# Decode attention over a sliding window: V of two slabs fetched by one DMA with 65536-byte rows, its products on 64 weight columns, and the second slab's softmax run at once

## The chip, the cores and the metric

The kernel runs on one core of one Trainium2 chip. The metric is the device time of one execution in microseconds (us). Before the change it is 362.82 us, the median of 3 runs (362.75 to 362.86). The profile shown here is of one execution of its own, which took 363.02 us.

## The reference, cut to what matters

Two independent problems A and B of the same shape are computed and their outputs laid side by side. Each is one decode step of attention with a sliding window.

```python
B, Sq, D = 2, 1, 576
Hq, Hkv, Sk, Dh = 32, 16, 16384, 128
W = min(4096, max(256, Sk // 4))                 # 4096: only the last 4096 keys count
q = (x @ wq).reshape(B, Sq, Hq, Dh).transpose(0, 2, 1, 3)
k = jnp.repeat(k_cache[:, :, Sk - W:, :], 2, axis=1)
v = jnp.repeat(v_cache[:, :, Sk - W:, :], 2, axis=1)
scores = jnp.einsum("bhqd,bhkd->bhqk", q, k) * (Dh ** -0.5)
p = softmax(scores, axis=-1)
o = jnp.einsum("bhqk,bhkd->bhqd", p, v)
return o.transpose(0, 2, 1, 3).reshape(B, Sq, Hq * Dh) @ wo
# out = concatenate([problem A, problem B], axis=-1)
```

All tensors are bf16. One head's window of K (or V) is 4096 x 128 x 2 bytes = 1 MiB, and each problem has 2 x 16 heads of K and as many of V, so 128 MiB of cache are read for one query row of each head. The rest that is read are wq and wo, 4.5 MiB each for each problem.

## The kernel before, in words

**Slabs and groups.** The work is cut into 16 slabs (ND, eight for each problem). A slab holds four heads, `[g::SPP]` of the 32 (line 246): 4 MiB of K and 4 MiB of V, each fetched by one DMA into one slot of the tile ring (128 partitions, four slots of 32768 bytes in a partition). A partition gets 128 consecutive positions times 128 elements of one head, which are 32768 consecutive bytes of the cache: one row of the DMA. Two slabs, 2G and 2G+1, make a group G.

**The stream.** All large transfers are issued by SP, in the order of the list stream (lines 216 to 223), and each waits for the reader of the slot that it overwrites (`reader[n - NR]`, four transfers back). SP issues in order, so a transfer that waits holds up those behind it. Before, the order is Q0, Q1 (the wq of the two problems), K0, K1, V0, K2, V1, ..., K13, V12, K14, K15, V13, V14, V15. V15 comes in two pieces (PIECES: 3 MiB and 1 MiB). wo comes in parts that are issued ahead of a named transfer (w_at, line 226): part 0 (all of problem A) ahead of K5, part 1 ahead of V11, part 2 ahead of V12; part 3 and the small last pieces (issue_last) behind V15.

**One slab.** The names of the steps are those of the code, with s for the slab and u = 0..3 for a quarter of it:

- X(s,u), DVE, line 515: a transpose of a quarter of the K slab into xt, which has NKT = 3 buffers; X(s,u) therefore waits for the S that read the buffer three quarters ago. X(s,3) frees the slot of K.
- S(s,u), PE, lines 540 and 188: eight matmuls of 512 columns into the scores' PSUM tile ST[s % 2], which ACT has filled with a mask before (fill, line 415).
- max, Tm, nM, nMrep, bias, bcp, exp (lines 550, 553, 563, 568, 573, 579, 585): the maximum of the slab, turned and spread by two tiny PE transposes, then one ACT exponential into pR, with the sums in rsum.
- pC, DVE, line 593: a transpose of pR into the weights of the V product. It waits for fill(s+2) and exp(s).
- PV, PE, line 631: 32 matmuls of 512 columns, each with 32 weight columns (128 x 32 of the array), four of them on the four column quarters of the array at a time, into ACC. It needs V of the slab and pC.
- rsel (POOL), tot (PE), rsb (DVE): 1/sum of a group. accev (ACT, line 643), accm, acca, accr (POOL), comb (PE), norm, spread (DVE): fold ACC into the group's output. redist, rev, proj (PE, ACT, PE, lines 739, 757, 786): the product with wo.

**The order within an engine** is the order in which the loop at lines 849 to 890 adds the steps; every engine works strictly in that order. In it, the softmax of slab s-1 is laid between the quarters of slab s: max(s-1) behind X(s,0), Tm behind S(s,0), nM ahead of X(s,2), bias and exp ahead of X(s,3), pC(s-1) behind X(s,3), PV(s-1) behind S(s,3). S(s,3) waits for pC(s-1) (line 529). After the loop (lines 891 to 923) come the last slab's softmax between pieces of PV13, then PV14, comb, norm and proj of group 6 in two steps, PV15 in its two pieces, and the output.

**The start.** wq of both problems arrives, the queries of all eight groups are computed (q, qrow, qtr, qkeep), and only then X(0,0) runs, since DVE does the qtr of all groups first.

Of the kernel before, what the change touches and what calls it, by code (L numbers as in the profile page):

```python
# [59 lines left out]
def build_kernel(nc, probs, out, cfg=None):  # L60
    cfg = dict(cfg or {})
    NR = cfg.get("NR", 4)
    NKT = cfg.get("NKT", 3)
    NPT = cfg.get("NPT", 3)
    LS = 1
# [48 lines left out]
    with es:  # L114
# [25 lines left out]
        pR = sb("pR", [128, 1024], BF16)  # L140
        pC = sb("pC", [128, NPT, NJ, 8], BF16)
# [22 lines left out]
        acc_r = sb("acc_r", [128, 2, 128], BF16)  # L164
        o_rest = sb("o_rest", [Bb, NB1], FP32)
        ident_r = sb("ident_r", [128, 32], BF16)
        out_A = sb("out_A", [Bb, NOUT], BF16)
        out_sb = [out_A[:, :], pR[0:Bb, 0:NOUT]]
# [11 lines left out]
        wo_sem = [sem("wo%d" % r) for r in range(2)]  # L180
# [30 lines left out]
        p_zq = S.add("dve", lambda e: e.memset(zq[:].rearrange("d p z w -> d (p z w)").bitcast(FP32), 0.0), [], "zero_zq")  # L211
        p_ones_f = S.add("dve", lambda e: e.memset(ones_f[:], 1.0), [], "ones_f")
# [4 lines left out]
        for s_ in range(ND + LS):  # L217
            if s_ < ND:
                stream.append(("K", s_))
            if s_ >= LS and s_ != ND - 2:  # L220
                if s_ == ND - 1:
                    stream.append(("V", ND - 3))
                stream.append(("V", s_ - LS))
        pos = {key: n for n, key in enumerate(stream)}
        w_at = {}
        for part, at in ((0, ("K", 5)), (1, ("V", 11)), (2, ("V", 12))):
            w_at.setdefault(at, []).append(part)

        slab_dma = {}
# [9 lines left out]
        def issue_slab(n):  # L239
# [4 lines left out]
            P, g = D_ // SPP, D_ % SPP  # L244
            src_t = probs[P][1] if kind == "K" else probs[P][2]
            src = src_t.rearrange("b h s d -> (b h) s d")[g::SPP, Sk - W:Sk, :].rearrange("c (r j) d -> r c (j d)", r=32)
            r = n % NR
            deps = [reader[n - NR]] if n >= NR else []
# [10 lines left out]
        def issue_wq(n, P):  # L259
            wqP = probs[P][3]  # L260
            r = n % NR
            deps = [reader[n - NR]] if n >= NR else []
# [9 lines left out]
        def issue_last(woP, lo, r0, deps):  # L272
            for n_, hs in enumerate(HEADS):
                def f(e, n_=n_, hs=hs):
                    t, r = divmod(hs[0], 2)
                    row = t * HH + r0 + 256 + 128 * r
                    return e.dma_start(wob[:, lo + 4 + hs[0]:lo + 4 + hs[0] + len(hs), :],
                                       woP[row:row + 128 * len(hs), :].rearrange("(h d) n -> d h n", d=128)).then_inc(wl_sem[n_], 16)
                wo_last.append(dma_op("sp", wl_sem[n_], 1, f, deps, "wl%d" % n_))

        def issue_wo(part):
# [3 lines left out]
                (16, 8, 1024, 1, [proj.get(5)], (6,)),  # L285
                (24, 4, 1536, 1, [proj.get(7)], (7,)))[part]
            assert None not in deps
            woP = probs[P][4]
            sem_ = wo_sem[lo // 16]
            src = woP.rearrange("(t r) n -> t r n", t=2)[:, r0:r0 + 64 * n, :].rearrange("t (p s) n -> p t (s n)", s=n)  # L290
# [4 lines left out]
            if part == 3:  # L295
                issue_last(woP, lo, r0, deps)
# [48 lines left out]
        def init_small():  # L345
# [15 lines left out]
                mask4S[:], ident_b[:].rearrange("d (a s) -> d s a", s=4), AX.X, ALU.max), [p_ident_b], "mask4S")  # L361
            init["maskJ"] = S.add("dve", lambda e: e.tensor_reduce(
# [48 lines left out]
        def do_fill(s):  # L411
            deps = [init["maskB"], zqev[s]]
# [11 lines left out]
        def do_qpair(i):  # L424
# [14 lines left out]
            for g in range(2):  # L439
                def fn(e, part=todo_[(0, ends[0])[g]:ends[g]]):  # L440
                    last = None
                    for ch, b in part:
                        c0 = (b % 2) * HH + 512 * (Gs[b // 2] % GPP)
                        w_ = ring[:, nq % NR, ch * HD + c0:ch * HD + c0 + 512] if ch < NFC else wqr[:, P, c0 - (b % 2) * HH:c0 - (b % 2) * HH + 512]
# [63 lines left out]
        def do_X(s, u):  # L508
# [4 lines left out]
            if i >= NKT:  # L513
# [3 lines left out]
                ring[:, n % NR, :].bitcast(FP32).rearrange("k (j q w) -> k q j w", q=4, w=64)[:, u]),  # L517
# [4 lines left out]
        def do_S(s, u):  # L522
# [5 lines left out]
            if u == NU - 1 and 1 <= s < ND - 1:  # L528
                deps.append(chain[(s - 1, "pC")])
# [42 lines left out]
        def do_exp(s):  # L572
# [8 lines left out]
            if s >= 1:  # L581
                d.append(chain[(s - 1, "pC")])
            if s >= 2:
                d.append(chain[(s // 2 - 1, "rsel")])
            chain[(s, "exp")] = S.add("act", lambda e: e.activation(  # L585
                pR[:, :], ST[s % 2][:, :], ACTF.Exp, bias=bias_sb[:, 0:1], scale=SCALE,
                accum_out=rsum[:, s % 2:s % 2 + 1]), d, "exp%d" % s)

        def do_pC(s):
            d = [chain.get((s + 2, "fill")), chain[(s, "exp")]]  # L590
            if s >= NPT:
                d.append(PVop[s - NPT])
            chain[(s, "pC")] = S.add("dve", lambda e: e.transpose(  # L593
                pC[:, s % NPT, :, :].rearrange("k j c -> k (j c)"), pR[:, :]), d, "pC%d" % s)

        def do_rsel(G):
            d = [chain[(2 * G, "exp")], chain[(2 * G + 1, "exp")], init["maskS"]]
# [20 lines left out]
        def do_PV(D_, rounds, wait):  # L618
# [4 lines left out]
            if rounds[0] == 0 and D_ >= 1:  # L623
                deps.append(acc_ev[D_ - 1])

            def f(e):
                last = None
                for jr in rounds:
                    for cb in range(4):
                        j0_ = JR * jr + 4 * cb  # L630
                        last = e.matmul(ACC[32 * cb:32 * cb + 32, 0:512],  # L631
                                        pC[:, D_ % NPT, j0_:j0_ + 4, :].rearrange("k j c -> k (j c)"),
                                        ring[:, n % NR, j0_ * 128:(j0_ + 4) * 128],
# [5 lines left out]
            if rounds[-1] == last_r:  # L639
                d = [op]  # L640
                if D_ >= 2:
                    d.append(acc_r_ev[D_ - 2])
                acc_ev[D_] = S.add("act", lambda e: e.activation(acc_sb[:, D_ % 2, :], ACC[:, :], ACTF.Copy), d, "accev%d" % D_)  # L643
                G = D_ // 2
                if not by_group(G) or (D_ % 2 == 0 and G < NG - 2):
                    return
                l0, l1 = (0, 2) if G < NG - 2 else (D_ % 2, D_ % 2 + 1)
                a_ = acc_sb[:, l0:l1, :]
                v = a_.rearrange("k l (j d) -> k l j d", j=4)
                t = S.add("pool", lambda e: e.tensor_tensor(  # L650
                    v, v, maskJ[:].unsqueeze(1).unsqueeze(3).broadcast_to([128, l1 - l0, 4, 128]), ALU.mult),
                    [acc_ev[2 * G + l] for l in range(l0, l1)] + [init["maskJ"]], "accm%d" % D_)
                t = S.add("pool", lambda e: e.tensor_tensor(a_[:, :, 0:256], a_[:, :, 0:256], a_[:, :, 256:512], ALU.add),  # L653
                          [t], "acca%d" % D_)
                d = [t]
                if G >= 1:
                    d.append(comb[2 * G - 1])
                t = S.add("pool", lambda e: e.tensor_tensor(
                    acc_r[:, l0:l1, :], a_[:, :, 0:128], a_[:, :, 128:256], ALU.add), d, "accr%d" % D_)
                for l in range(l0, l1):  # L660
                    acc_r_ev[2 * G + l] = t

        def do_comb(D_):
            if by_group(D_ // 2):
# [3 lines left out]
                def fg(e, bank):  # L668
                    last = None
                    for l_ in range(2):  # L670
                        last = e.matmul(bank[:, 8 * l_:8 * l_ + 8], acc_r[:, l_, :], maskS[:, :], start=True, stop=True)
                    return last
                n, bank, comb[D_] = tb_job(fg, "comb%d" % D_, [acc_r_ev[D_ - 1], acc_r_ev[D_], init["maskS"]])
# [10 lines left out]
        def do_norm(D_):  # L684
# [5 lines left out]
            if by_group(G):  # L690
# [3 lines left out]
                def f_nm(e):  # L694
                    last = None
                    for l_ in range(2):
                        last = e.tensor_tensor(
                            oTg[u % 2][:, 0:16 * nG].rearrange("d (b g l r t) -> d g l b t r", b=Bb, g=nG, l=2, r=2)[:, G - g0, l_],
# [6 lines left out]
                nk, mD = {4: (4, "maskA"), 2: (8, "mask16D"), 1: (16, "maskD")}[nG]  # L705
                mask_ = {"maskA": maskA, "mask16D": mask16D, "maskD": maskD}[mD]
                deps = [norm[D_], init[mD]]
                if u >= 2:
                    deps.append(redist[u - 2])
                spread[u] = S.add("dve", lambda e: e.tensor_tensor(  # L710
                    om[:, u % 2, :].rearrange("d (h k t) -> d h k t", k=nk, t=2),
# [312 lines left out]
```

## Time and profile before

| what | value |
|---|---|
| median of 3 runs | 362.82 us |
| the profiled execution | 363.02 us |
| its span, first to last instruction | 361.8 us |
| time around the span | 363.02 - 361.8 = 1.2 us |
| bytes read | 153.10 MB |
| busy: PE, DVE, ACT, POOL | 60%, 56%, 19%, 10% |
| mean granted TensorE clock | 0.882 |

How to read it: busy times are shares of the span; the row DMA of the page gives in 40 slices of 9.05 us how busy the core's 16 DMA engines were, in tenths. In a timeline a row is: start in us, length in us, engine, line, operation, tiles, shapes and count, and in brackets the idle time of the engine just before it and what ended that idle time. The chain of waits is the sequence of steps that ended last, followed back from the last instruction. Matmuls overlap, so that rows of one matmul each start about 0.22 us apart at full clock and about 0.43 us apart at half clock, though each lasts 0.38 us or 0.63 us.

### The profile page before, as it was taken

What the parts mean: (1) busy time and instruction counts of PE and PEld (TensorE: products, weight loads), DVE (VectorE), ACT (ScalarE), POOL (GpSimd) and SP (SyncE); (2) the same over time, 40 slices, a digit from 0 to 9 for tenths busy, and PEclk for the clock granted to TensorE, in tenths of its full rate; (3) what the DMA queues carried; (4) which work ended last, traced back from release to release, by engine and by line L of the source; (5) the groups of instructions that cost most, each with busy time, mean ns of one, the idle gap of its engine ahead of it and who ended that gap; (6) DMA issues with size and microseconds to landing.
All of it is one profiled execution on the core that took longest, in us unless ns stands there. A gap on an engine that the chain in (4) does not pass through costs nothing.

```text
span 361.8 us, 2730 instructions
## 1 busy us (share of the span) xinstructions
PE 218.6 (60%) x1318; PEld 55.8 (15%) x945; DVE 200.9 (56%) x175; ACT 68.2 (19%) x149; POOL 35.3 (10%) x55
## 2 busy tenths in 40 slices
PE   0399195763747207466574737766867707657786
PEld 0010021120111101112120201212121201211132
DVE  4112599846647019283756658392919239079931
ACT  1036502130203002103020203020201203002131
POOL 1000000004000400001300040002100040200020
PEclk9999689997889857969698978899898978969999
DMA  8999999999999999999999999999999999999996
GB/s 348 421 449 406 464 406 437 431 408 453 415 442 438 428 424 438 429 428 438 417 446 422 435 428 442 426 435 428 424 424 440 431 424 433 431 438 428 438 409 248
DMA packets 6491, 153.27 MB, mean 424 GB/s; under 512 B 712, under 2 KB 1232, under 8 KB 1616
## 3 DMA queue, kind: packets, MB, share of 16 engines
q1 hardware_dynamic: 6476, 153.10, 98.8%
q8 instruction: 9, 0.15, 0.2%
q14 instruction: 2, 0.02, 0.0%
q10 hardware_dynamic: 4, 0.00, 0.0%
HBM read 153.10 MB, written 0.00 MB: 423 GB/s over the span
## 4 chain that ended last, share of the span: by engine, by line
DMA 72%; DVE 17%; PE 7%; ACT 3%; SPq 1%; issue 0%
DMA ring<-in_B_k_cache_dram 34%; DMA ring<-in_A_k_cache_dram 27%; DVE xt L515 14%; DMA wob<-in_B_wo_dram 8%; DMA wob<-in_B_x_dram 3%; PE st L188 3%; PE st L540 3%; ACT wob L465 1%; DVE wob L475 1%; ACT qk L483 1%; PE st L450 1%; DVE m L550 1%; ACT wob L470 1%; DVE nM L563 0%; SPq L252 0%
## 5 line engine op out<-in xcount | busy, mean ns | idle before, releaser
L515 DVE STREAM_TRANSPOSE xt<-ring 128x2048 f32<-128x2048 f32 x64 | 145.3, 2284 | 86.6 <-DMA ring<-in_A_k_cache_dram 49.8
L540 PE MATMUL st<-xt,zq 128*128 128x512 bf16 x256 | 111.6, 436 | 122.6 <-DVE xt L515 98.1
L188 PE MATMUL st<-xt,zq 128*128 128x512 bf16 x256 | 110.1, 430 | 0.0
L540 PEld LDWEIGHTS st<-xt,zq 128*128 128x128 bf16 x256 | 27.1, 106 | 216.3 <-DVE xt L515 113.5
L631 PE MATMUL acc<-ring,pC 128*32 128x512 bf16 x512 | 32.5, 381 | 1.2 <-DMA ring<-in_B_v_cache_dram 1.2
L568 ACT ACTIVATE nMrep<-nM 1x128 f32<-1x128 f32 x16 | 4.9, 308 | 146.9 <-DVE nM L563 146.9
L643 ACT ACTIVATE acc_sb<-acc 128x512 bf16<-128x512 f32 x16 | 9.5, 596 | 79.9 <-PE acc L631 79.9
L593 DVE STREAM_TRANSPOSE pC<-pR 128x1024 bf16<-128x1024 bf16 x16 | 19.6, 1223 | 3.7 <-ACT pR L585 2.1
L650 POOL TENSOR_TENSOR acc_sb<-acc_sb,masks 128x1024 bf16<-128x1024 bf16 (+1 forms) x8 | 13.4, 1679 | 66.6 <-ACT acc_sb L643 66.6
L550 DVE TENSOR_REDUCE m<-st 128x1 f32<-128x1024 f32 x16 | 19.0, 1190 | 1.4 <-PE st L188 1.4
L502 POOL TENSOR_TENSOR zq<-qk,masks 128x128 bf16<-128x128 bf16 x16 | 6.3, 398 | 136.2 <-PE st L188 114.4
L585 ACT ACTIVATE pR<-st,bias_sb 128x1024 bf16<-128x1024 f32 x16 | 17.8, 1114 | 0.5
L475 DVE STREAM_TRANSPOSE wob<-wob 128x512 f32<-128x512 f32 x8 | 5.7, 711 | 20.3 <-ACT wob L465 12.9
L415 ACT ACTIVATE st<-maskB 128x1024 f32<-128x1024 bf16 x16 | 16.5, 1032 | 1.6 <-POOL rsel L600 0.4
L786 PE MATMUL ot<-wob,Rsb 128*2 128x512 bf16 x56 | 15.2, 390 | 0.0
L631 PEld LDWEIGHTS acc<-ring,pC 128*32 128x32 bf16 x512 | 12.4, 96 | 15.9 <-issue 3.2
L600 POOL TENSOR_TENSOR rsel<-masks,rsum 128x16 f32<-128x16 bf16 x8 | 1.7, 216 | 108.0 <-ACT pR L585 108.0
L188 PE MATMUL tb<-wob,Rsb 128*2 128x64 bf16 x56 | 10.9, 195 | 0.0
L375 PE MATMUL tb<-wob 4*128 4x16 bf16 x5 | 0.3, 179 | 14.5 <-DVE wob L380 14.5
L653 POOL TENSOR_TENSOR acc_sb<-acc_sb 128x512 bf16<-128x512 bf16 (+1 forms) x8 | 8.2, 1029 | 0.6
L188 PE MATMUL st<-ring,wob 128*128 128x512 bf16 x24 | 7.9, 445 | 0.0
L579 ACT ACTIVATE bias_sb<-tb 128x1 f32<-128x1 f32 x16 | 2.7, 171 | 24.8 <-PE tb L573 24.8
(89 smaller groups left out, 99.5 us busy)
## 6 DMA issues: line engine op xcount, KB each, us to landing
ring<-in_A_k_cache_dram SPq DMA_DIRECT2D x8, 4096.0 KB, 30.4
ring<-in_A_v_cache_dram SPq DMA_DIRECT2D x8, 4096.0 KB, 32.5
ring<-in_B_k_cache_dram SPq DMA_DIRECT2D x8, 4096.0 KB, 28.4
ring<-in_B_v_cache_dram SPq DMA_DIRECT2D x7, 4096.0 KB, 32.8
wob<-in_A_wo_dram SPq DMA_DIRECT2D x1, 4608.0 KB, 43.3
ring<-in_A_wq_dram SPq DMA_DIRECT2D x1, 4096.0 KB, 12.7
ring<-in_B_wq_dram SPq DMA_DIRECT2D x1, 4096.0 KB, 22.6
ring<-in_B_v_cache_dram SPq DMA_DIRECT2D x1, 3072.0 KB, 25.5
```

The costliest lines, as they stand in the source:

```text
L188: return e.add_instruction(mybir.InstMatmult(name=nc.get_next_instruction_name(), engine=i.engine, ins=[e.lower_ap(rhs), i.ins[1]], outs=[ ...
L415: chain[(s, "fill")] = S.add("act", lambda e: e.activation(ST[s % 2][:, :].rearrange("k (h j) -> k h j", h=2), maskB[:].unsqueeze(1).broad ...
L475: chain[(G, "qtr")] = S.add("dve", lambda e: e.transpose(qtr[:].bitcast(FP32), qrow[:].bitcast(FP32)), evs, "qtr%d" % G)
L515: Xop[(s, u)] = S.add("dve", lambda e: e.transpose(xt[:, i % NKT, :].rearrange("k (j w) -> k j w", w=64), ring[:, n % NR, :].bitcast(FP32) ...
L540: first = last = e.matmul(bank, zq[:, p4, s % NZQ, w0:w0 + 128], mv, start=False, stop=stop, skip_group_check=True)
L550: chain[(s, "max")] = S.add("dve", lambda e: e.tensor_reduce(m1[:, 0:1], ST[s % 2][:, :], AX.X, ALU.max), d, "max%d" % s)
L585: chain[(s, "exp")] = S.add("act", lambda e: e.activation(pR[:, :], ST[s % 2][:, :], ACTF.Exp, bias=bias_sb[:, 0:1], scale=SCALE, accum_ou ...
L593: chain[(s, "pC")] = S.add("dve", lambda e: e.transpose(pC[:, s % NPT, :, :].rearrange("k j c -> k (j c)"), pR[:, :]), d, "pC%d" % s)
L631: last = e.matmul(ACC[32 * cb:32 * cb + 32, 0:512], pC[:, D_ % NPT, j0_:j0_ + 4, :].rearrange("k j c -> k (j c)"), ring[:, n % NR, j0_ * 1 ...
L643: acc_ev[D_] = S.add("act", lambda e: e.activation(acc_sb[:, D_ % 2, :], ACC[:, :], ACTF.Copy), d, "accev%d" % D_)
L650: t = S.add("pool", lambda e: e.tensor_tensor(v, v, maskJ[:].unsqueeze(1).unsqueeze(3).broadcast_to([128, l1 - l0, 4, 128]), ALU.mult), [a ...
L786: first = e.matmul(OT[0:Bb, 0:NB0], l_, wob[:, w0 + s_, 0:NB0], start=start and begin, stop=end, skip_group_check=True)
```

## The change

**The stream.** K keeps to ring slots 0 and 1, and slots 2 and 3 (at the start the two wq) take V of a whole group: VV(G), one DMA of 8 MiB, whose partition holds 65536 consecutive bytes of one head. The order becomes Q0, Q1, K0, K1, VV0, K2, K3, VV1, ..., K12, K13, VV6, K14, K15, V14, V15; the last group is fetched as before. Each transfer waits for the reader of what stood in its slots: VV(G+1) for the product of VV(G), K(s+2) for X(s,3). wo's parts stand ahead of VV1, VV5 and V14. Slab 2G+l of a problem takes the heads g+4l, g+4l+8, ... (g the group within the problem), so that a group holds every fourth head, and VV(G) fetches eight heads, 16 rows of 65536 bytes from each.

**The products.** PVV(G) does both slabs of a group in one step: 64 matmuls of 512 columns with 64 weight columns each (32 of either slab, the positions that belong to the other slab are zero), two at a time on the two column halves of the array. pR gets 2048 columns for a slab, of which exp writes one interleaved half, and the other half stays zero from one memset at the start; pC becomes a transpose of 128 x 2048 instead of 128 x 1024 (for slabs 14 and 15 it stays 128 x 1024). accev, accm, acca and accr run once for a group, on 512 columns. A new mask, maskL, serves comb.

**The order.** For an even slab the softmax is laid between the quarters of the next slab, as before. For an odd slab it runs at once, behind S(s,3): max, Tm, nM, bias, exp, fill(s+2), pC, then rsel, proj where one is due, tot, rsb and PVV(G). NKT goes from 3 to 2. S(s,3) no longer waits for pC(s-1); rsel waits for pC instead of exp. comb, norm, spread and redist of group G-1 lie in the even slab of group G. The proj steps move to slabs 8 to 13 and 15. After the loop there are only PV14, comb, norm, the two pieces of PV15 and the end.

The core of the diff:

```diff
-    NKT = cfg.get("NKT", 3)
-    NPT = cfg.get("NPT", 3)
-    LS = 1
+    NKT = cfg.get("NKT", 2)
...
-        pR = sb("pR", [128, 1024], BF16)
-        pC = sb("pC", [128, NPT, NJ, 8], BF16)
+        pR = sb("pR", [128, 2, 2048], BF16)
+        pC = sb("pC", [128, NJ // 2, 2, 32], BF16)
...
+        p_zpR = S.add("pool", lambda e: e.memset(pR[:].rearrange("k l n -> k (l n)").bitcast(FP32), 0.0), [], "zero_pR")
...
-        for s_ in range(ND + LS):
-            if s_ < ND:
-                stream.append(("K", s_))
-            if s_ >= LS and s_ != ND - 2:
-                if s_ == ND - 1:
-                    stream.append(("V", ND - 3))
-                stream.append(("V", s_ - LS))
+        for s_ in range(ND):
+            stream.append(("K", s_))
+            if s_ % 2 and s_ < ND - 1:
+                stream.append(("VV", s_ // 2))
+        stream += [("V", ND - 2), ("V", ND - 1)]
+        slots_of = lambda kind, i: {"Q": (2 + i % 2,), "K": (i % 2,), "VV": (2, 3), "V": (2 + i % 2,)}[kind]
+        held_by = {}
+        before_ = []
+        for n_, key in enumerate(stream):
+            before_.append(sorted({held_by[r] for r in slots_of(*key) if r in held_by}))
+            for r in slots_of(*key):
+                held_by[r] = n_
+        slot = [slots_of(*key)[0] for key in stream]
...
-        for part, at in ((0, ("K", 5)), (1, ("V", 11)), (2, ("V", 12))):
+        for part, at in ((0, ("VV", 1)), (1, ("VV", 5)), (2, ("V", ND - 2))):
...
+        vv = ring[:, 2:4, :].rearrange("k a n -> k (a n)")
...
+            deps = [reader[n_] for n_ in before_[n]]
+            if kind == "VV":
+                vsrc = probs[D_ // GPP][2].rearrange("b h s d -> (b h) s d")[D_ % GPP::GPP, Sk - W:Sk, :].rearrange(
+                    "x (r j) d -> r x (j d)", r=16)
+                slab_dma[n] = dma_op("sp", ring_sem[r], 1, lambda e: e.dma_start(vv, vsrc).then_inc(ring_sem[r], 16), deps, "VV%d" % D_)
+                return
+            P, g = D_ // SPP, D_ % SPP // 2 + GPP * (D_ % 2)
...
-            if u == NU - 1 and 1 <= s < ND - 1:
-                deps.append(chain[(s - 1, "pC")])
...
+            l = s % 2
+            if s < ND - 2:
+                d.append(p_zpR)
+                o_ = pR[:, l, :].rearrange("k (h n x) -> k h n x", h=2, x=8)[:, :, :, l::2]
+                i_ = ST[l][:, :].rearrange("k (n h c) -> k h n c", h=2, c=4)
+            else:
+                o_, i_ = pR[:, l, 0:1024], ST[l][:, :]
...
+                d.append(PVop[2 * (s // 2) - 1])
+            nj = NJ // 2 if s < ND - 2 else NJ // 4
             chain[(s, "pC")] = S.add("dve", lambda e: e.transpose(
-                pC[:, s % NPT, :, :].rearrange("k j c -> k (j c)"), pR[:, :]), d, "pC%d" % s)
+                pC[:, 0:nj, s % 2, :], pR[:, s % 2, 0:32 * nj].rearrange("k (j w) -> k j w", w=32)), d, "pC%d" % s)
...
-            d = [chain[(2 * G, "exp")], chain[(2 * G + 1, "exp")], init["maskS"]]
+            d = [chain[(2 * G, "pC")], chain[(2 * G + 1, "pC")], init["maskS"]]
...
+        def do_PVV(G):
+            n = pos[("VV", G)]
+            issue_until(n)
+            D_ = 2 * G + 1
+            deps = [slab_dma[n], chain[(D_ - 1, "pC")], chain[(D_, "pC")], acc_free[0]]
+            if G:
+                deps.append(acc_ev[D_ - 2])
+
+            def f(e):
+                last = None
+                for jg in range(2 * NJ // 4):
+                    cb = jg % 2
+                    last = e.matmul(ACC[64 * cb:64 * cb + 64, 0:512],
+                                    pC[:, jg, :, :].rearrange("k l w -> k (l w)"),
+                                    vv[:, 512 * jg:512 * jg + 512],
+                                    start=jg < 2, stop=jg >= 2 * NJ // 4 - 2)
+                return last
+            op = S.add("pe", f, deps, "PVV%d" % G)
+            PVop[D_] = op
+            reader[n] = op
...
+            acc_ev[D_] = S.add("act", lambda e: e.activation(a_, ACC[:, :], ACTF.Copy), d, "accev%d" % D_)
...
+        proj_at = {8: 0, 9: 1, 10: 2, 11: 3, 12: 4, 13: 5, 15: 6}
...
         for s in range(ND):
-            D2 = s - 2
+            odd = s % 2
             c = s - 1
+            G = s // 2
             for u in range(NU):
-                if c >= 0:
+                if odd:
                     if u == 2:
                         do_nm2(c)
                     elif u == 3:
                         do_exp(c)
                         if c + 2 < ND:
                             do_fill(c + 2)
+                if odd and u == 0:
+                    do_max(c)
                 do_X(s, u)
-                if c >= 0:
-                    if u == 0:
-                        do_max(c)
-                        if c % 2 == 0 and c >= 2:
-                            do_rsb(c // 2 - 1)
-                    elif u == 3:
-                        do_pC(c)
+                if odd and u == 3:
+                    do_pC(c)
                 if u >= 1:
                     do_S(s, u - 1)
-                if u == 1 and 1 <= s < ND - 1:
+                if odd and u == 1 and s < ND - 1:
                     do_zq(s + 1)
-                if c >= 0 and u == 1:
+                if odd and u == 1:
                     do_nm(c)
-                if D2 >= 0 and D2 % 2 == 1 and s < ND - 1:
+                if not odd and G:
                     if u == 2:
-                        do_comb(D2)
-                        do_norm(D2)
-                    elif u == 3 and s - 2 in redist_at:
-                        do_redist(redist_at[s - 2])
+                        do_comb(s - 1)
+                        do_norm(s - 1)
+                    elif u == 3 and G - 1 in redist_at:
+                        if s == ND - 2:
+                            issue_until(pos[("V", s)])
+                        do_redist(redist_at[G - 1])
             do_S(s, NU - 1)
-            if s in proj_at:
-                do_proj(2 * proj_at[s] + 1)
-                if proj_at[s] == GPP - 1:
-                    do_E(0)
-            if c >= 0:
-                if c % 2 == 1:
-                    do_rsel(c // 2)
-                    do_tot(c // 2)
-                if s < ND - 2:
-                    do_PV(c, range(NRD), None)
-        s = ND - 1
-        D_ = ND - 3
-        do_max(s)
-        do_PV(D_, range(0, 2), None)
-        do_nm(s)
-        do_nm2(s)
-        do_PV(D_, range(2, 4), None)
-        do_exp(s)
-        do_rsel(s // 2)
-        do_pC(s)
-        do_PV(D_, range(4, NRD), None)
-        do_tot(s // 2)
-        do_rsb(s // 2)
+            if not odd:
+                proj_of(s)
+                continue
+            do_max(s)
+            do_nm(s)
+            do_nm2(s)
+            do_exp(s)
+            if s + 2 < ND:
+                do_zq(s + 2)
+                do_fill(s + 2)
+            do_pC(s)
+            do_rsel(G)
+            proj_of(s)
+            do_tot(G)
+            do_rsb(G)
+            if s < ND - 1:
+                do_PVV(G)
         do_PV(ND - 2, range(NRD), None)
-        do_comb(D_)
-        do_norm(D_)
-        do_proj(2 * 5 + 1)
-        do_redist(2)
         do_comb(ND - 2)
         do_norm(ND - 2)
-        do_proj(D_)
         D_ = ND - 1
         issue_until(len(stream) - 1)
         do_PV(D_, range(PIECES[0][0] // JR, PIECES[0][1] // JR), pieces[0])

```

## The prediction

> **What bounds the kernel now.** I read the page first (its DMA row and the shares of the chain), then the chain of waits, then the timelines of DVE and PE.
>
> ```profile
> DMA  8999999999999999999999999999999999999996
> ...
> DMA 72%; DVE 17%; PE 7%; ACT 3%; SPq 1%; issue 0%
> ```
>
> The DMA engines are at nine tenths or more in 38 of 40 slices: the queue never runs dry. So the end is the time to move 153.1 MB plus what is left to do behind the last byte. The chain shows that rest:
>
> ```profile
> 281.28 36.61 DMA ring<-in_B_k_cache_dram
> ...
> 331.87 27.84 DMA wob<-in_B_wo_dram
> 359.71 0.04 issue
> 359.75 0.31 PE st L790 x2
> ```
>
> The last piece of wo is there at 359.71, and 2.1 us later the span ends (361.8). The first transposes of K slabs in the same chain give the speed of the stream:
>
> ```profile
> 65.08 2.31 DVE xt L515
> ...
> 104.28 2.32 DVE xt L515
> ...
> 154.11 2.32 DVE xt L515
> ...
> 193.14 2.32 DVE xt L515
> ...
> 232.05 2.31 DVE xt L515
> ...
> 270.76 2.32 DVE xt L515
> ```
>
> Each start is the landing of an even K slab (K2, K4, ...). Two K and two V (16.78 MB) take 39.20, 39.03, 38.91 and 38.71 us, mean 38.96: 9.74 us a slab, 431 GB/s. The stretch from 104.28 to 154.11 holds wo's part 0 besides: 49.83 - 38.96 = 10.87 us for 4.72 MB.
>
> **The change, part by part.** The sum is made against the span of 361.8 us; the profiled execution took 363.02, the median is 362.82, so 0.2 us go off at the end. Differences under 0.2% (0.73 us) are no difference to a measurement here.
>
> *Rows of 65536 bytes.* Before, 14 slabs of V cost each DMA engine 8 rows apiece (128 rows over 16 engines), 112 in all; after, 56. No row here is that long, so I look for a price per row. wo has 8 rows per engine in each part too, of 36864, 18432 and 9216 bytes. They take 10.87 us; 295.70 - 270.76 - 19.48 = 5.46 us; 317.92 - 295.70 - 19.48 = 2.74 us (starts of X(12), X(13), X(14), less a K and a V). A line through the three has a slope of 2.297 us per MB and 0.03 us left for 8 rows; by that slope a slab of 4.194 MB would take 9.63 us, and it takes 9.74: 0.11 us for 8 rows. So a row costs 0.004 to 0.013 us, and 56 fewer save 0.2 to 0.7 us. The other ends: nothing (9216-byte rows move no slower than 36864-byte ones), and 1.1 us if V moved at the 434 GB/s of part 0. I take -0.4.
>
> *Does the stream stay full?* Take the landing of an even K as zero; then odd K lands at 9.7 and VV at 29.2. X takes 2.3 and then 2.2 us, S 1.9 us (7 x 0.217 + 0.38). NKT = 2 makes X(s,2) wait for S(s,0): X(even,3) ends at 9.8, S(even,3) at 11.7, max 12.9, X(odd,0) 15.2, X(odd,3) 22.0, pC(even) at twice its 1.2 us 24.3, max(odd) 25.5, exp 28.3, fill 29.3, pC(odd) 31.6, rsel and tot 32.3. PVV starts there, 3.1 us after its V landed. Before, 32 matmuls on quarters of the array took 1.91 us:
>
> ```profile
> 188.28 1.91 PE L631 MATMUL acc<-ring,pC 128*32 128x512 bf16 x32
> ```
>
> That is 8 rounds 0.217 us apart and 0.38. PVV has 64 on two halves, 32 rounds: 31 x 0.217 + 0.38 = 7.1 us, 8.8 if its first 3.4 us run at half clock. So the next VV is asked for at 39.4 to 42.4, while the queue holds two K until 29.2 + 19.5 = 48.7: a reserve of 6 us or more. The engines' own cycle is 7.1 + (32.3 - 2.4) = 37.0 us, at worst 40 with both half-clock starts, against 39 of supply; wo's parts 0 and 1 give 10.9 and 5.5 us back. At the start VV0 is asked for at about 36 (K2 is asked for at 36.04 on the same products), with K1 in the queue until 25.05 + 19.5 = 44.5; VV1 at about 82, with part 0 queued until 94. The cost along the stream is therefore 0, and PE's 7 x 3.3 us more hide in its idle time (40% of the span). The memset of pR and maskL stand ahead of x, for which DVE waits until 14.2. If that cover failed, the reserve above is what would go first.
>
> *The end.* This is where the path changes. Before, three V slabs and 1.18 MB of wo follow K15; after, part 2 of wo, two V and the same rest. With K14's landing as zero the last byte lands at 9.74 (K15) + 2.74 + 19.48 + 2.84 = 34.8, and before at 359.71 - 317.9 = 41.8. So the engines lose 7 us. They now do less behind the last softmax (no PV13, no proj of group 5), but not 7 us less. By the recurrence above, with pC(14) at its single length, S(15,3) ends at 24.0. What follows has rows in the end of before:
>
> ```profile
> 342.44 1.23 DVE L550 TENSOR_REDUCE m<-st 128x1 f32<-128x1024 f32 x1 [0.88 <-PE st L188]
> ...
> 346.39 1.25 DVE L593 STREAM_TRANSPOSE pC<-pR 128x1024 bf16<-128x1024 bf16 x1 [2.09 <-ACT pR L585]
> ```
>
> S(15,3) ended at 342.40 and pC(15) at 347.64: 5.2 us. rsel, which now waits for pC, and tot add 0.7 (24.0 + 5.9 = 29.9); proj of group 6 (2 us) lies beside that. PV14 1.9, accev 0.65, comb 0.2, PV15's 32 matmuls 1.9 (its first piece landed at 29.5, the second at 32.0): 34.5. From there before took 2.3 us to the end of the last proj where no DMA held it (357.48 to 359.10, and 0.66) and 1.7 to the end of the span: 38.5, where the last byte plus 2.1 is 36.9. So **+1.6 us** at full clock.
>
> The clock decides on more. From S(14,3)'s end to S(15,0) PE idles for max and X(15,0), 3.5 us, with no proj between (slab 14 has none). Such gaps before:
>
> ```profile
> 225.12 0.39 PE L540 MATMUL st<-xt,zq 128*128 128x512 bf16 x1 [1.99 <-DVE pC L593]
> ```
> ```profile
> 253.71 0.61 PE L540 MATMUL st<-xt,zq 128*128 128x512 bf16 x1 [3.88 <-DVE xt L515]
> ```
>
> After 1.99 us the matmuls are at full clock (0.39), after 3.88 at half (0.61, 0.43 apart). The ends are 0 and a half-clock S(15,0) of 3.4 us; with Tm and nM behind it X(15,2) then starts at 18.9 instead of 17.6: +1.3. I take 1.3, since 3.5 is nearest to 3.88.
>
> [...]
>
> exp writes 1024 of 2048 columns with a stride: between its 1.11 us and twice that; off the end, since slabs 14 and 15 write as before. I take 1.11.
>
> **Sum.** -0.4 + 1.6 + 1.3 = +2.5 us: span 364.3, profiled execution 365.5, median 365.3.
>
> **Rivals.**
> - *Full clock at the end:* -0.4 + 1.6 = +1.2: 364.0. Speaks for it: the gap is short of 3.88 us. Chance 0.25, the forecast itself 0.33.
> - *The transfer still ends last:* my chain at the end is some 2 us too long (DVE and PE overlap more), and only the rows count: 362.8 - 0.2 to 0.7, so 362.1 to 362.6. For it: before, proj of group 6 ended at 354.2 and V15's first piece landed at 354.4, so that end was matched too. Chance 0.20.
> - *Faster, V moves better in long rows:* V at 434 GB/s or above, 1.1 us less: 361.7. It decides only if S(15,3) ends by 22.4 on the scale above, where the engines' lag of 1.6 is gone. Against it: 9216-byte rows already run as fast. Chance 0.10.
> - *Slower stream from the address pattern.* Beside a bound unknown to this trace, V's 136 us (14 x 9.74) cost 1.4 us for each per cent lost: at 3% 362.8 + 4.1 + 1.6 = 368.5. [...] Chance 0.06. [...]
> - *The halves of the array don't run side by side:* PVV takes 14 us, the cycle 44 us against 39, five late groups: some 20 us, 385. The quarters do run side by side. Chance 0.06.
>
> **How the numbers follow.** Slower by over 0.2%: 0.33 + 0.25 + 0.06 + 0.06 = 0.70, of which a part of the first two (a chain 1 us shorter than I count) goes to "same": 0.66. Same: 0.20 + 0.04 = 0.24. Faster: 0.10. The range runs from near the fast end of the third case, 362.2, to 368.0, short of the stream's loss of 3%; outside lie the last case, most of the pattern case, and most of the faster one, 0.2 in all.
>
> **What would show it.** Right: the DMA row stays at 9 to the last slice; 896 packets fewer; no X or PVV late by over some 4 us; behind K15 the engines, not wo's last piece, end the chain, with DVE and PE of slabs 14 and 15 in it. PVV rows of about 7 us confirm the halves. Wrong: a slice of the DMA row under 9 in the middle (the reserve is gone), PVV of 14 us, K landings of a group over 39.5 us apart (V slower) or under 38 (V faster), or the chain ending in the landing of wo again.

## The result, and the profile after

The changed kernel takes **525.26 us**, the median of 6 runs (521.71 to 557.3), against 362.82 us (362.75 to 362.9) before. The ratio is 1.445, with a 95% interval of 1.44 to 1.45. The interval leaves out the run of 557.3, which is slower than the other five by 6%. The profiled execution took 521.71 us, its span is 520.0 us. The forecast was 365.3 us, the range 362.2 to 368.0.

These are the rows of the page of after: the busy share of the DMA engines and what they moved, by slices of 13 us, the packets, and the chain by engine.

```profile
DMA  8999979999999999899998999999999899989994
GB/s 363 444 423 302 242 163 316 429 422 198 212 189 396 358 187 223 209 441 287 212 197 279 459 197 207 198 363 420 266 203 217 310 416 208 202 184 413 430 418 191
DMA packets 5483, 153.27 MB, mean 295 GB/s; under 512 B 600, under 2 KB 1120, under 8 KB 1504
...
another core or an unknown queue 32%; DVE 28%; PE 19%; DMA 11%; ACT 8%; issue 1%; SPq 0%; POOL 0%; ACTq 0%
```

The first row is nearly the row of before: nines to the end. Read alone it says that nothing happened. The second row says what did: the rate swings between some 440 and some 200 GB/s, with the engines nearly as busy. Busy is the time that packets take, whatever they bring in it: in the windows below a share of 1.02 goes with 210 GB/s and one of 1.03 with 442. Three stretches by windows (length, then busy time of PE, PEld, DVE, ACT and POOL with instruction counts, granted TensorE clock, share of the DMA engines, GB/s):

```profile
50.00:60.00 10.00, 6.18 (x23) 1.17 (x11) 7.51 (x4) 0.00 (x0) 0.40 (x1) 0.88 1.02 210
140.00:150.00 10.00, 0.00 (x0) 0.00 (x0) 0.00 (x0) 0.00 (x0) 0.00 (x0) 0.50 1.02 210
160.00:170.00 10.00, 8.04 (x60) 3.55 (x56) 1.97 (x1) 0.60 (x1) 1.16 (x2) 0.83 1.03 442
```

The first two lie in VV0 and VV1, the third in K4. V comes at 210 GB/s, K at 442, and from 140 to 150 no engine of the core does anything at all, so it is not the engines that hold V up. The waits say the same (line and what it waited for: us in total, times, longest):

```profile
DVE xt L532 <- DMA ring<-in_B_k_cache_dram: 101.7, 4, 28.7
DVE xt L532 <- DMA ring<-in_A_k_cache_dram: 81.6, 3, 36.8
...
PE acc L677 <- DMA ring<-in_A_v_cache_dram: 70.5, 4, 27.6
```

K is late too, mainly because it stands behind V in the queue. The first X of an even slab starts when its K lands, and these rows of the chain give nearly the whole loss:

```profile
168.03 2.32 DVE xt L532
...
229.32 2.32 DVE xt L532
...
290.64 2.32 DVE xt L532
```

They lie 61.3 us apart, where a group took 38.96 before. That is some 22.3 us more in a group and **156 us** in seven, of the 159 between the two profiled executions. Seven transfers of 8.39 MB at 210 GB/s take 7 x 39.9 us; at the 431 GB/s of before they would take 7 x 19.5. So the half rate of V makes 143 us. The other 13, 1.9 us in a group, fall where the rows of V and of K are under way together: K's packets of 32768 bytes, 1.22 us each in the median, take up to 2.66 us there. What is left to explain is why V runs at half rate.

### The profile page after: what moved, and what is told of

Same layout as the page of the kernel before. It is cut to its first block, busy times and chain, and to the rows that moved or that the text cites. A ratio compares the mean times of both kernels' runs of the same rounds, so it can differ in the third digit from the quotient of the medians.

```text
span 520.0 us, 2713 instructions
## 1 busy us (share of the span) xinstructions
PE 263.2 (51%) x1317; PEld 76.8 (15%) x945; DVE 217.9 (42%) x176; ACT 67.6 (13%) x142; POOL 25.8 (5%) x53
## 4 chain that ended last, share of the span: by engine, by line
another core or an unknown queue 32%; DVE 28%; PE 19%; DMA 11%; ACT 8%; issue 1%; SPq 0%; POOL 0%; ACTq 0%
DVE xt L532 17%; DMA ring<-in_A_k_cache_dram 8%; PE st L187 7%; PE st L555 7%; DVE pC L615 5%; DVE m L565 3%; ACT pR L606 3%; DMA wob<-in_B_wq_dram 2%; ACT st L430 2%; PE ot L829 2%; DVE wob L492 1%; PE tb L627 1%; ACT qk L500 1%; ACT wob L487 1%
## 5 line engine op out<-in xcount | busy, mean ns | idle before, releaser
L677 PE MATMUL acc<-ring,pC 128*64 128x512 bf16 x448 | 65.7, 466 | 119.0 <-DMA ring<-in_A_v_cache_dram 70.5
L677 PEld LDWEIGHTS acc<-ring,pC 128*64 128x64 bf16 x448 | 29.6, 133 | 152.5 <-DMA ring<-in_A_v_cache_dram 70.9
L615 DVE STREAM_TRANSPOSE pC<-pR 128x2048 bf16<-128x2048 bf16 (+1 forms) x16 | 34.8, 2175 | 28.3 <-ACT st L430 26.1
L689 ACT ACTIVATE acc_sb<-acc 128x512 bf16<-128x512 f32 x7 | 4.2, 597 | 207.7 <-PE acc L677 207.7
L606 ACT ACTIVATE pR<-st,bias_sb 128x1024 bf16<-128x1024 f32 x16 | 21.9, 1370 | 0.5
L627 PE MATMUL tb<-rsel,ones_f 128*128 128x16 f32 x16 | 4.9, 385 | 31.5 <-POOL rsel L622 31.5
L691 POOL TENSOR_TENSOR acc_sb<-acc_sb,masks 128x512 bf16<-128x512 bf16 x7 | 7.3, 1040 | 194.4 <-ACT acc_sb L689 194.4
L568 PE MATMUL tb<-ident_f,m 128*1 128x128 f32 x16 | 5.1, 316 | 13.9 <-DVE m L565 13.9
L578 DVE TENSOR_REDUCE nM<-tb 1x8 f32<-1x128 f32 x16 | 4.5, 278 | 14.0 <-PE tb L568 14.0
L627 PEld LDWEIGHTS tb<-rsel,ones_f 128*128 128x128 f32 x16 | 4.0, 312 | 33.7 <-POOL rsel L622 33.7
```

What stands on the lines that cost most here:

```text
L606: chain[(s, "exp")] = S.add("act", lambda e: e.activation(o_, i_, ACTF.Exp, bias=bias_sb[:, 0:1], scale=SCALE, accum_out=rsum[:, s % 2:s % ...
L615: chain[(s, "pC")] = S.add("dve", lambda e: e.transpose(pC[:, 0:nj, s % 2, :], pR[:, s % 2, 0:32 * nj].rearrange("k (j w) -> k j w", w=32) ...
L627: n, bank, op = tb_job(lambda e, bank: e.matmul(bank[:, 0:16], ones_f[:, :], rsel[:].rearrange("k l c -> k (l c)"), start=True, stop=True) ...
L677: last = e.matmul(ACC[64 * cb:64 * cb + 64, 0:512], pC[:, jg, :, :].rearrange("k l w -> k (l w)"), vv[:, 512 * jg:512 * jg + 512], start=j ...
L691: t = S.add("pool", lambda e: e.tensor_tensor(v, v, maskJ[:].unsqueeze(2).broadcast_to([128, 4, 128]), ALU.mult), [acc_ev[D_], init["maskJ ...
```

## The experiments

All kernels are the changed kernel with one more edit, unless another is named. At first three theories stood for the half rate: the length of the rows (65536 bytes), the amount in one transfer (8 MiB), and the pattern of addresses. A fourth came up as these fell.

### Half rows: 32768 bytes, nothing else

```diff
-  e.dma_start(vv, vsrc)
+  for lo, hi in ((0, SLABW), (SLABW, 2 * SLABW)):
+      e.dma_start(vv[:, lo:hi], vsrc[:, :, lo:hi])
```

> VV(G) is fetched by two DMAs, each with one half of every partition's 65536 bytes: rows of 32768 bytes whose starts still lie 65536 bytes apart, everything else as after the change. Theory L (a row of 65536 bytes moves at half speed, by its length): V is back at about 430 GB/s and what is left is the engines' lag at the end, 364 to 366 us. Theory P (starts 64 KiB apart collide in memory): still about 210 GB/s in V, some 520 us. Theory A (8 MiB in one DMA is too much): 364 to 366 us as well.

Measured: 518.19 us median of 6 runs (510.38 to 539.5), ratio 1.425 (1.421 to 1.430). The window inside VV1 of this kernel:

```profile
140.00:150.00 10.00, 0.00 (x0) 0.00 (x0) 0.00 (x0) 0.00 (x0) 0.00 (x0) 0.50 0.98 210
```

Rows of the length that ran at 430 GB/s before now run at 210, in transfers of 4 MiB as before. Length and amount both fall as causes.

### One transfer of 8 MiB, cut into 32 blocks instead of 16

```diff
-  "x (r j) d -> r x (j d)", r=16)                  # 16 blocks x 8 heads x 65536 bytes
-  e.dma_start(vv, vsrc)
+  "(c a) (r j) d -> r c a (j d)", a=2, r=32)       # 32 blocks x 4 heads x 2 x 32768 bytes
+  e.dma_start(ring[:, 2:4, :], vsrc)
```

The same bytes are read, but they land in other partitions than the products expect, so the output is another.

> VV(G) stays one DMA of 8 MiB into the same two slots, but with rows of 32768 bytes, two for each partition from two heads (V lands in other places than the products take it for, so the output is another; the time is what counts). Theory L: about 430 GB/s in V, 364 to 366 us. Theory A (amount in one DMA): 210 GB/s in V, some 520 us.

Measured: 376.98 us (one run, span 375.3). V is at full speed again:

```profile
GB/s 336 447 440 419 426 447 428 409 454 389 444 438 437 416 440 440 428 416 430 440 412 438 384 416 447 435 410 456 421 426 444 349 421 444 423 417 433 420 216 2
```

So 145 of the 159 us went with the cut. What is left, 14 us above before, is the engines' cycle. The changed kernel doesn't show it, since there the transfers of a group take longer, 61.3 us. This chain of waits runs through one group, from one V product to the next, and meets no DMA:

```profile
118.15 9.76 PE acc L677 x32
...
143.48 0.43 PE st L187
...
145.77 1.47 ACT pR L606 x2
147.32 1.04 ACT st L430
148.38 2.31 DVE pC L615
...
153.30 1.45 ACT pR L606 x2
154.83 1.04 ACT st L430
155.89 2.32 DVE pC L615
...
159.16 9.73 PE acc L677 x64
```

From 118.15 to 159.16 are 41.0 us, and the stream needs 38.96.

### Rows at another distance

```diff
-  [D_ % GPP::GPP, Sk - W:Sk, :].rearrange("x (r j) d -> r x (j d)", r=16)
+  [D_ % GPP::GPP, Sk - 16 * 272:Sk, :].rearrange("x (r j) d -> r x (j d)", r=16)[:, :, 0:2 * SLABW]
```

Rows start 69632 bytes apart instead of 65536, and V's contents are others.

> VV(G) stays one DMA with rows of 65536 bytes, but the rows of a head start 69632 bytes apart (other positions of V are read, so the output is another). Theory L: 210 GB/s in V as after the change, some 520 us. [...]

Measured: 522.35 us (one run), 210 GB/s from 50 to 60 us. The rows' distance being a power of two is not the cause; the distance of the heads stayed as it was. The 4 KiB more from one row to the next changed nothing: 522.35 us, where the changed kernel has 525.26.

### Seven lengths

Each group's rows are cut in two, the first part 40960, 45056, 49152, 53248, 57344, 61440 and 64512 bytes long.

```diff
+  cut = 128 * (160, 176, 192, 208, 224, 240, 252)[D_]
+  for lo, hi in ((0, cut), (cut, 2 * SLABW)):
+      e.dma_start(vv[:, lo:hi], vsrc[:, :, lo:hi])
```

> VV(G) is cut into two DMAs whose first has rows of 40960, 45056, 49152, 53248, 57344, 61440 and 64512 bytes in groups 0 to 6, and whose second has the rest. Theory L with a threshold at 64 KiB itself: every group at about 430 GB/s, 364 to 367 us. Theory L with a speed that falls steadily beyond 32 KiB or from some length on: the groups with longer first rows take longer, the slow part at 210 GB/s costing 13 us in group 0 to 20 us in group 6, up to some 480 us if all are slow; the first group that takes over 45 us instead of 39 (without wo) marks the length.

Measured: 519.29 us (one run), and all seven groups are at the low rate, the first at 213 GB/s from 50 to 60 us. No length is a threshold. The 480 us expected for seven slow groups took the second parts to be fast; these shorter rows, which have the same cut, are slow too.

### Seven forms of the source

Two theories were left, both about the cut. **The split:** a source of 16 blocks x 8 rows costs half the rate, whatever the addresses. By it forms 0, 1, 2 and 6 below are fast and 3, 4 and 5 slow. **The memory:** the addresses that are read at the same time collide. Each group got another source, as its expectation lists:

```diff
+  0: "(c a) (r j) d -> r c a (j d)", a=2, r=32      # 32 x 4 x 2 x 32768 bytes
+  1: "c (r j) d -> r c (j d)", r=32                 # 32 x 4 x 65536
+  2: "(p j) d -> p (j d)", p=128                    # 128 x 65536, dense
+  3: "r (x j) d -> r x (j d)", x=8                  # 16 x 8 x 65536, all but dense
+  4: eight transfers of 16 x 65536, to vv[16 * x:16 * x + 16, :]
+  5: "x (r j) d -> x r (j d)", r=16                 # 8 x 16 x 65536
+  6: "x (r j) d -> r x (j d)", r=64                 # 64 x 2 x 65536
```

> Each of the seven V transfers is given another form of its source, all of 8 MiB, with the rest of the kernel as changed (V's contents are others, so the output is too). By number of V transfer: 0 is 32 blocks of rows x 4 heads x 2 rows of 32768 bytes; 1 is 32 blocks x 4 heads, rows of 65536 bytes; 2 is one dense stretch of 8 MiB, 128 rows of 65536; 3 is 16 blocks x 8 rows of 65536 inside one head, the blocks 528384 bytes apart; 4 is eight transfers of one head and 16 rows each; 5 is 8 heads x 16 rows, the head outermost; 6 is 64 blocks x 2 heads of 65536. [...] Theory of the memory (heads 64 MiB apart read at the same time cost half the rate): 3 runs at about 430 like 2, 0 and 1 (4 heads) at 430, 6 not told. Theory of the 65536-byte row, which the runs so far speak against: 1, 2, 3, 6 all at about 210.

The heads of a transfer lie 16 MiB apart, and not 64 as the expectation has it. Measured: 528.95 us (one run). One window inside each of the seven, in order; the ends of the windows of forms 1, 2 and 6 can hold some K:

```profile
50.00:60.00 10.00, 6.18 (x22) 1.14 (x10) 6.52 (x5) 0.00 (x0) 0.40 (x1) 0.83 1.03 439
95.00:105.00 10.00, 7.48 (x26) 1.56 (x14) 8.56 (x5) 2.75 (x5) 0.00 (x0) 0.83 0.97 419
130.00:140.00 10.00, 5.78 (x27) 1.34 (x14) 8.00 (x7) 0.00 (x0) 0.40 (x1) 0.91 1.11 478
190.00:200.00 10.00, 1.82 (x9) 0.40 (x4) 6.01 (x4) 2.95 (x5) 0.48 (x2) 0.81 1.01 210
250.00:260.00 10.00, 5.63 (x25) 1.59 (x13) 5.51 (x5) 2.95 (x5) 0.62 (x2) 0.83 1.02 118
395.00:405.00 10.00, 0.00 (x0) 0.00 (x0) 0.00 (x0) 0.00 (x0) 0.00 (x0) 0.50 0.51 105
450.00:460.00 10.00, 5.14 (x32) 1.34 (x15) 5.95 (x6) 0.20 (x1) 0.40 (x1) 0.95 1.05 454
```

Forms 1 and 2 bring rows of 65536 bytes at full speed (419 and 478 GB/s). Form 3 reads almost the same addresses as form 2 and runs at 210; its source differs in having 16 blocks of 8 rows and not 128 rows. The share column tells form 5 from form 4: form 4 has a share of 1.02 at 118 GB/s, form 5 one of 0.51 at 105. If 0.51 stands for eight engines that work all the time, each brings 13 GB/s, where 431 over sixteen are 27.

The numbers fit one picture, an inference from the rates: what counts is in how many different places of the tile the rows land that are under way at one time. Each transfer of form 4 goes to 16 neighbouring partitions, 118 GB/s here and 107 from 265 to 275 us. The change and form 3 send 16 blocks to eight neighbouring partitions each, 210 GB/s. The sources with 32, 64 and 128 blocks ran at 419 to 478. Which engine writes which partition, and what would hold up neighbours, no view shows.

### The same reads, landing apart

To part landing from reading, this kernel keeps the reads of form 4 and changes only where they land. If the landing counts, V is faster than in form 4; if the reads do, it is not.

```diff
+  for x in range(8):                                # one head each: 16 rows of 65536 bytes
+      e.dma_start(vv[x::8, :], vsrc[x])
```

> The changed kernel with each V transfer of seven groups cut into eight, one for each head: 16 rows of 65536 bytes to partitions x, x+8, x+16, ... It reads the same kind of addresses as transfer 4 of the seven-forms run (which went to 16 neighbouring partitions and ran at 107 to 118 GB/s), and computes the reference's output. [...] Theory of the memory (the addresses read at the same time set the rate): V runs at 107 to 118 GB/s as in transfer 4, 7 x 38 us more, near 790 us.

Measured: 522.38 us (one run). In VV0 and VV1:

```profile
50.00:60.00 10.00, 6.12 (x23) 1.25 (x12) 7.83 (x4) 0.00 (x0) 0.40 (x1) 0.91 1.02 210
...
140.00:150.00 10.00, 0.00 (x0) 0.00 (x0) 0.00 (x0) 0.00 (x0) 0.00 (x0) 0.50 0.99 203
```

Transfers of 16 rows of one head ran at 107 to 118 GB/s into 16 neighbouring partitions, and at 203 to 210 into 16 partitions that lie 8 apart. The same kind of reads, another landing, nearly twice the rate: the theory of the memory falls. Eight heads in one transfer or in eight make no difference either (525.26 us and 522.38).

### The split alone, in the kernel before

```diff
 (kernel before)
+  if kind == "V":
+      src = src_t....[D_ % 4::4, Sk - W // 2:Sk, :].rearrange("x (r j) d -> r x (j d)", r=16)
```

> The kernel before, with one edit: each V slab is fetched as 16 blocks x 8 heads in rows of 32768 bytes instead of 32 blocks x 4 heads (half the positions of twice the heads, so V's contents are others and so is the output). Amount, row length, order, products and waits are those of before. Theory of the split: V runs at about 210 GB/s, each of 16 slabs takes 20.0 instead of 9.75 us, so 362.8 + 16 x 10.2 = about 526 us. If the length of the rows, the size of the transfer or the order is needed for the loss: about 363 us.

Measured: 630.07 us (one run). The split by itself, with rows, amounts, order and products of before, makes the kernel slower still: 104 us more than expected. The windows show where:

```profile
50.00:60.00 10.00, 8.06 (x38) 1.84 (x19) 9.81 (x7) 1.89 (x5) 0.40 (x1) 1.00 1.01 210
...
240.00:250.00 10.00, 8.01 (x32) 1.65 (x16) 8.41 (x6) 2.71 (x5) 0.22 (x1) 0.90 0.99 210
```

Half of all bytes in this stretch are K's, cut into 32 blocks as ever, and yet the rate hardly leaves 210 after the first 270 us (the page's row has 203 to 267 in its slices of 15.7 us from the 18th on, bar the last two). So here K is slowed as well. The run of the seven forms shows such a case. Form 5 alone has a share of 0.51 (395 to 405 us); while the K slabs asked for behind it come in as well, the share is more than twice that:

```profile
365.00:375.00 10.00, 0.00 (x0) 0.00 (x0) 0.00 (x0) 0.00 (x0) 0.00 (x0) 0.50 1.12 157
```

The two kinds together bring 157 GB/s at a share of 1.12, where form 5 alone brought 105 and K's form, in the window of K4, 442. From 345 to 385 us they bring 131 to 157. So a transfer that is fast by itself is slowed by a slow one under way with it, as K's packets were in the changed kernel (1.22 us in the median, up to 2.66 beside V's rows). That this makes the 104 us is likely but was not tested by itself, and where the two hold each other up was not shown.

### The other 14 us: a clock, the products, the order

First the half clock. This is the kernel of the second experiment (V lands elsewhere) with 25 matmuls more in each odd slab's softmax, to fill PE's idle time there. They write to the accumulator that the products then overwrite.

```diff
+  for _ in range(count):                            # 5, 4 and 16 of them, around Tm and bias
+      e.matmul(ACC[:, :], maskB[:, 0:128], maskB[:, :], start=True, stop=True)
```

> As the run with one transfer in 32768-byte rows from 32 blocks (V lands elsewhere, so the output is another), with 25 more 128x512 matmuls on PE in the odd slab's softmax, written to the accumulator that the products then overwrite. If the half clock at the start of the double product (9.7 us for 64 matmuls) is what makes the cycle 41.0 us, the product takes about 7.1 us, the cycle comes to 38.4 to 39 and the time to about 366 us. If the cycle is set elsewhere, it stays at 41.0 and the time at about 377 us or above.

Measured: 368.11 us (one run), 9 us less with more work. The chain has the product at

```profile
238.98 7.03 PE acc L688 x64
```

and the DMA row is full but for the last slice. Of the four products in the chain three take these 7.03 us, the one at 158.31 takes 8.71. The time is still 2 us above the 366 expected. The distance from one VV issue to the next is uneven here, 38 to 43 us, since the queue is the bound again.

Then the order by itself: the second slab's softmax at once, but V by slab and 32 weight columns as before. And the same with V of both slabs in one transfer, cut into 32 blocks:

```diff
 (changed kernel, products and pC as before the change)
+  stream += [("V", s_ - 1), ("V", s_)]              # order alone
```
```diff
+  stream.append(("VV", s_ // 2))                    # order and one transfer
+  "(c a) (r j) d -> r c a (j d)", a=2, r=32
```

> The softmax of the second slab at once as in the changed kernel, but V by slab in 32768-byte rows and products with 32 weight columns as before: the order alone. The products split in two of 32 matmuls that wait for one slab's V each, so the cycle should fit the 39 us that the transfers need: V at about 430 GB/s, and 363 to 366 us, against 525 for the whole change. If the order itself costs the half rate of the V transfers, V stays at about 210 GB/s and the time above 500 us.

> The order-alone kernel with V of both slabs of seven groups in one transfer of 8 MiB, as 32 blocks x 4 heads x 2 rows of 32768 bytes; products by slab with 32 weight columns. It computes the reference's output. If one transfer of 8 MiB is harmless by itself, V runs at about 430 GB/s and the time is 366 to 370 us (the products of a group now wait for all 8 MiB, at the end of the cycle, so up to 3 us more than the order alone). If the size of the transfer matters, the rate in V falls below 400 GB/s.

Measured: the order alone 366.91 us, median of 4 runs (365.76 to 368.52), ratio 1.0099 (1.0081 to 1.0118), just above the 363 to 366 expected. With one transfer 366.61 us (365.66 to 368.68), ratio 1.0122 (1.0082 to 1.0161): not to be told apart. The chain of the latter waits for K again, as before the change,

```profile
135.75 27.91 DMA ring<-in_A_k_cache_dram
...
172.75 29.77 DMA ring<-in_B_k_cache_dram
```

and ends with the engines: in the profiled execution of the order alone the chain has 32 matmuls of PV15 at 361.25 and the span ends at 366.9.

The parts of the change then stand like this:

| kernel | us | step |
|---|---|---|
| before | 362.8 to 362.9 | |
| order alone | 366.91 | +4.1 |
| and V of two slabs in one transfer, 32 blocks | 366.61 | -0.3, no difference |
| and 64 weight columns, pC and exp on 2048 | 376.98 | +10.4 |
| and 16 blocks x 8 heads (32768-byte rows 518, 65536-byte rows 525) | 518 to 525 | +141 to +148 |

The steps stand for this order of the edits. At half rate the transfers of a group outlast the engines' cycle, so the last step hides the +10.4 of the one before it.

## Why the prediction was wrong

**The step that failed** is "Rows of 65536 bytes". It asked what a row costs by its length, from wo's parts, and set ends of 0 and -1.1 us. The count was right (896 packets of V fewer; the other 112 that are gone are under 512 bytes), and the length does cost nothing (rows of 65536 bytes came at 419 to 478 GB/s in forms 1, 2 and 6). But the step priced the row and not the transfer: to get rows of 65536 bytes the source goes from 32 blocks x 4 heads to 16 x 8, and with it changes, as the rates suggest, where the rows land that are under way at one time. No row of before has that form, so the range should have had a bad end for it, as it should for anything that no row shows. The term is about +155 us, not -0.4. By the sum K14 lands 39.8 us before a span of 364.3 ends, at 324.5; it lands at 479.88. In the kernel with the order and one transfer of 32 blocks it lands at 324.6.

**The rival "slower stream"** had the place and the formula: 1.4 us for each per cent. It went wrong on cause and on size: the 3% was the author's estimate, and V lost half its rate (210 for 431 GB/s). It took the addresses read for the only pattern; K's rows, at full speed before, are of the form 32 x 4, and the landing side was not looked at. At half rate the formula gives 136 x (431 / 210 - 1) = 143 us, of some 155 measured.

**"The stream stays full" at no cost** is not put to the test in the changed kernel, where slow V outlasts the engines. With V at full speed it fails by 14 us. The cycle is 41.0 us and not 37.0 ("at worst 40"). Three sizes were short. PVV is 9.7 us and not 7.1 to 8.8: the half clock that PE falls into during the softmax lasts longer than the 3.4 us that I allowed, the length of a half-clock stretch of before (granted clock 0.50 from 195.10 to 198.50). In the changed kernel the product at 86.44 runs at 0.50 for its first 5.26 us. With PE kept busy a product is 7.03 us in three of the four groups of the chain. exp into the strided half is 1.40 us and not 1.11 (which the kernel with the order and one transfer, whose exp writes without a stride, still takes); the note that it costs nothing "off the end" overlooked that it lies on the cycle. And an S at half clock follows the odd slab's first X as well (0.43 us apart at 143.48). The halves of the array do run side by side: 7.03 us is 31 x 0.217 + 0.3. That rival is wrong.

**The end** came as forecast. From K14's landing the sum takes 38.5 us and 1.3 for a half clock, 39.8. In the changed kernel it is 520.0 - 479.88 = 40.1, and the engines end the chain:

```profile
479.88 6.70 DVE xt L532 x3
...
494.89 0.61 PE st L555
```

Ahead of the second row, S(15,0), PE was idle for 3.54 us, as the sum said, and the eight matmuls start 0.43 us apart: half clock. The rivals of a full clock there, and of a transfer that still ends last, are wrong. With the order and one transfer the end takes 364.0 - 324.6 = 39.4 us in the profiled execution. The order alone took 366.9 - 324.7 = 42.2 in its own; what sets the 2 us between the two was not looked for.

**What would show it:** the sign that I named, the DMA row at 9 to the last slice, all but held while the kernel lost 159 us. "K landings of a group over 39.5 us apart" was the right sign for V slower.

## What to carry to other kernels

When a DMA's shape changes, ask into which partitions its rows land together, not only how long they are: here 16 blocks x 8 rows ran at 210 GB/s where 32 x 4, 64 x 2 and 128 x 1 ran at 419 to 478, with the same amount. That the landing sets the rate is shown (107 to 118 GB/s against 203 to 210 for the same kind of reads); by what way it does is not. Read the GB/s row beside the DMA row, since a share of 1.02 stood beside 210 GB/s and one of 1.03 beside 442. And when the softmax is taken out of the shadow of the next slab, look for PE at half clock in it: here the product behind it took 9.7 us for 7.03.

## What the runs showed of the hardware beyond that

- With an outermost count of 8 (form 5) the DMA engines' share was 0.51 and the rate 105 GB/s from 395 to 405 us; 16 rows into 16 neighbouring partitions (form 4) ran at 107 to 118 GB/s at a share of 0.91 to 1.02.
- Slow and fast transfers didn't simply add up: with V at half rate in turn with K, slab by slab, the time was 630 us where the sum gave 526. Beside form 5, which ran at 105 GB/s by itself, K and V together brought 131 to 157.
- 25 matmuls of no use in each group made a kernel 9 us faster (376.98 to 368.11, one run each), by the granted clock that they keep up: its mean is 0.939 with them and 0.864 without.
- Behind 3.54 us of idle PE all of S(15,0) ran at half clock (0.43 us apart), as six matmuls did behind 3.88 us before the change. Behind the 1.99 us that the prediction set against it (225.12 before the change) only the first three matmuls are at full clock, and the granted clock is 0.50 from 225.79 to 229.20. In the changed kernel 2.30 us (231.68) were followed by half clock from the first matmul on and 3.12 us (421.17) by none. So the length of the gap alone did not decide.
